# First batch of a fused attention and two-expert-layer kernel: transposes first, the second weight matrix converted between the last pieces of the first, loads put behind the first product

## The chip, the cores and the metric

The kernel runs on 1 core of one Trainium2 chip. The metric is the device time of a run in microseconds; lower is better. The engines are written as the profile writes them: PE (TensorE), DVE (VectorE), ACT (ScalarE), POOL (GpSimd), SP (SyncE, which here only issues DMAs). Each engine works through its own list of instructions in order.

## The reference

Eight batches of 576 tokens go through a Nystrom attention (8 heads of 64, 32 landmarks), then through a dense layer with squared ReLU, then through a layer of 8 experts of which each token takes one:

```
q_lm, k_lm = means of q and k over 18 rows each          # 32 landmarks
A, Bm, C = softmax(q k_lm'), softmax(q_lm k_lm'), softmax(q_lm k')
Z = iterated inverse of Bm (6 rounds)
x = A @ Z @ C @ v                                         # 4608 x 512
h = relu(x @ w_in); x = (h * h) @ w_out                   # w_in 512 x 2048, w_out 2048 x 512
e = argmax(x @ w_gate)
out = softmax gate * sigmoid(x @ w_output_gate)[e] * (relu(x @ w1[e]) @ w2[e])
```

The inputs w_in, w_out, w1 and w2 arrive as 64-bit floats in DRAM.

## The kernel before

All large products are made with three matmuls of 32-bit operands: a high part times a high part, and two cross terms. A value is split into a high part (ACT copies it into the rounded type `F32R`) and a low part (DVE or POOL subtracts).

For each batch b the attention leaves a matrix A (`made`, split into `ab`) and a weight `wt` made from Z, C and v. `chunk` multiplies `wt` into w_in, a quarter of its columns at a time; the four products of a batch are called G (`gt`, tiles `gb`). `gemm(b)` then runs over two halves c of the batch's tokens (288 columns each) and over 16 slices f of the hidden width: six matmuls give `hp`, ACT makes `r = relu(hp)`, `gh` and `g` (both the square of r, one rounded, one not), DVE makes `gl = g - gh`, and `second` multiplies w_out's slice f (`wo`) with gh and gl: twelve matmuls into `acc`. `second` runs two slices behind `hp`.

Everything for batch 0 has to happen before that. `prologue` loads q and k (tiles `t`), makes their landmark sums (`sums`: on DVE, for the last tile on POOL, tile `st`), transposes q and k on PE (`transposed`, ACT copies the result to `x`), and runs the steps of `unit` for batch 0: landmarks (`lm`), scores, softmaxes (`ec`, `aa`), values, the powers of the inverse (`ee`, `ef`), the last values (`wz`) and `wt`. `first_g` then makes the first two G.

Between these steps `convert` turns w_in and w_out from 64 to 32 bits, in 16 pieces of 128 x 512 for each: a DMA fetches `raw` (four buffers), a cast makes the top half word `m` (on ACT or on POOL), ACT makes `r` from the low words, POOL adds the two in two halves into `wf` (w_in) or `w` (w_out). A piece of w_in is written back to DRAM (`win`) for the later batches. A piece of w_out is split as soon as it is converted: ACT copies, DVE subtracts, into `wo[f]`.

The steps of the next batch's attention run beside `gemm` as side work, `rate` steps for each of the four points of a slice; a scheduler at build time decides the order on each engine. It takes hints: `high_priority`, and `follow(a, b)`, which puts a behind b in the order without making it wait on the chip. The DMAs of loads and write-backs are issued by SP in order.

## Time and profile before

| | |
|---|---|
| time, median of 3 runs | 1259.56 us (1258.18 to 1260.97) |
| the profiled execution's own time | 1259.2 us |
| its span | 1257.5 us |
| PE busy | 1206.7 us, 96% of the span |
| DVE, ACT, POOL busy | 591.3, 615.2, 421.3 us |
| mean granted clock of PE | 0.978 of full speed |

The span is the time from the first to the last instruction; 1.7 us of the profiled execution lie around it. "Busy" is the time in which an engine had an instruction in work; waiting on another engine is not busy.

### The profile page before, as it was taken

How to read it: one execution, taken by the hardware profiler on the slowest of the kernel's cores; microseconds unless marked ns; L12 is line 12 of the kernel's file. 1: busy time of each engine (PE TensorE's matmuls, PEld its weight loads, DVE VectorE, ACT ScalarE, POOL GpSimd, SP SyncE). 2: the span in 40 equal slices, each digit the busy share in tenths (PEclk: the TensorE clock that was granted, in tenths of full speed). 3: DMA queues.
4: the chain of work that ended last, by engine and by line, in shares of the span. 5: the costliest groups of instructions: out<-in, count | busy, mean ns of one | idle time of the engine just before them, and what ended most of it. 6: DMA issues, size and time to landing. Idle time of an engine off the chain costs nothing.

```text
span 1257.5 us, 25149 instructions
## 1 busy us (share of the span) xinstructions
PE 1206.7 (96%) x9834; PEld 1078.6 (86%) x9834; DVE 591.3 (47%) x1498; ACT 615.2 (49%) x1433; POOL 421.3 (34%) x568
## 2 busy tenths in 40 slices
PE   4598999999999999999999999999999999999996
PEld 3377888989989989989989999998888888888885
DVE  5586466567547557556556332233333323323231
ACT  5586364564564564564564454553343433424331
POOL 5787514332233233232112000163342423424220
PEclk7699999999999999999999999999999999999998
DMA  9944333252152142141133210152534435343231
GB/s 339 336 164 135 124 122 109 91 168 61 59 171 64 53 158 77 53 158 58 54 120 108 69 37 2 39 151 84 143 105 139 129 115 159 108 125 110 90 96 40
DMA packets 88408, 142.24 MB, mean 113 GB/s; under 512 B 6430, under 2 KB 61758, under 8 KB 84702
## 3 DMA queue, kind: packets, MB, share of 16 engines
q1 hardware_dynamic: 87854, 139.97, 34.4%
q8 instruction: 79, 1.29, 0.4%
q0 software_dynamic: 288, 0.43, 0.1%
q14 instruction: 43, 0.35, 0.1%
q10 hardware_dynamic: 144, 0.20, 0.0%
HBM read 117.47 MB, written 23.11 MB: 112 GB/s over the span
## 4 chain that ended last, share of the span: by engine, by line
PE 90%; DVE 3%; DMA 3%; ACT 2%; POOL 1%; issue 1%; SPq 0%; POOLq 0%; ACTq 0%; DVEq 0%
PE acc L402 32%; PE hp L402 32%; PE y L402 17%; PE two L398 4%; PE bank L398 2%; PE bank L410 1%; DMA raw<-in_moe_w_in_dram 1%; PE pl L398 1%; DMA v<-in_v_dram 1%; PE pt L1168 1%; DVE x L488 1%; DMA t<-in_q_dram 1%; DVE gl L1079 1%; ACT r L185 0%; DVE ma L559 0%
## 5 line engine op out<-in xcount | busy, mean ns | idle before, releaser
L402 PE MATMUL acc<-gh,wo 128*128 128x288 f32 x2048 | 453.5, 299 | 7.7 <-ACT wo L218 5.0
L402 PEld LDWEIGHTS acc<-gh,wo 128*128 128x128 f32 x2048 | 341.1, 189 | 30.0 <-ACT gh L1077 8.4
L402 PE MATMUL acc<-gl,wo 128*128 128x288 f32 x1024 | 288.9, 298 | 1.1 <-DVE gl L1079 1.1
L402 PE MATMUL hp<-ab,gb 128*128 128x288 f32 x1536 | 255.7, 301 | 1.6 <-ACT r L1076 1.5
L402 PEld LDWEIGHTS hp<-ab,gb 128*128 128x128 f32 x1536 | 216.0, 189 | 21.3 <-issue 11.8
L1076 ACT ACTIVATE r<-hp 128x288 f32<-128x288 f32 x256 | 105.4, 412 | 256.0 <-PE hp L402 254.4
L1079 DVE TENSOR_TENSOR gl<-g,gh 128x288 fp32r<-128x288 f32 x256 | 131.4, 514 | 198.8 <-ACT g L1078 192.6
L402 PE MATMUL y<-s,h 128*128 128x512 f32 (+1 forms) x896 | 223.0, 396 | 0.8 <-ACT h L1311 0.5
L402 PEld LDWEIGHTS hp<-xs,s 128*128 128x128 f32 x1536 | 212.2, 188 | 7.5 <-DVE ls L1522 0.3
L402 PE MATMUL hp<-xs,s 128*128 128x288 f32 x1536 | 217.1, 295 | 0.2 <-DVE ls L1522 0.2
L402 PEld LDWEIGHTS acc<-gl,wo 128*128 128x128 f32 x1024 | 193.4, 189 | 4.0 <-DVE gl L1079 3.0
L402 PEld LDWEIGHTS y<-s,h 128*128 128x128 f32 (+1 forms) x896 | 160.6, 184 | 37.7 <-ACT h L1311 0.7
L230 POOL TENSOR_TENSOR s<-r,s 128x256 fp32r<-128x256 f32 x128 | 102.0, 819 | 234.8 <-ACT s L218 234.8
L1311 ACT ACTIVATE h<-hp 128x288 fp32r<-128x288 f32 x128 | 52.6, 412 | 186.8 <-PE hp L402 172.6
L1314 DVE SCALAR_TENSOR_TENSOR h<-hp,h 128x64 fp32r<-128x64 f32 (+2 forms) x192 | 62.6, 354 | 166.3 <-ACT h L1311 165.9
L1077 ACT ACTIVATE gh<-r 128x288 fp32r<-128x288 f32 x256 | 114.2, 446 | 12.5 <-PE acc L402 5.8
L1078 ACT ACTIVATE g<-r 128x288 f32<-128x288 f32 x256 | 110.6, 432 | 5.3 <-DVE gl L1079 5.0
L218 ACT CAST s<-r 128x512 fp32r<-128x512 f32 x128 | 77.6, 617 | 71.4 <-PE y L402 56.1
L499 POOL COPY x<-x 32x576 f32<-32x576 f32 x48 | 33.9, 706 | 195.7 <-DVE x L488 102.7
L224 DVE TENSOR_TENSOR s<-r,s 128x512 fp32r<-128x512 f32 x64 | 50.9, 795 | 103.3 <-ACT s L218 103.3
L230 POOL TENSOR_TENSOR xs<-xr,xs 128x576 fp32r<-128x576 f32 x32 | 45.9, 1459 | 64.0 <-ACT xs L218 48.0
L444 POOL TENSOR_TENSOR st<-t 128x288 f32<-128x288 f32 x50 | 40.7, 835 | 75.1 <-DMA t<-in_q_dram 73.1
(198 smaller groups left out, 1097.7 us busy)
## 6 DMA issues: line engine op xcount, KB each, us to landing
r<-in_moe_w_dram SPq DMA_DIRECT2D x128, 256.0 KB
wi<-win SPq DMA_DIRECT2D x28, 1024.0 KB
t<-in_k_dram SPq DMA_DIRECT2D x16, 576.0 KB
t<-in_q_dram SPq DMA_DIRECT2D x16, 576.0 KB
v<-in_v_dram SPq DMA_DIRECT2D x32, 288.0 KB
x_d<-x SPq DMA_DIRECT2D x16, 576.0 KB
xr<-x_d SPq DMA_DIRECT2D x16, 576.0 KB
raw<-in_moe_w_in_dram SPq DMA_DIRECT2D x16, 511.8 KB
```

What stands on the lines that cost most here:

```text
L218: hi = self.nc.scalar.copy(out=t[:, 0], in_=raw)
L224: lo_eng.tensor_tensor(out=t[:, 1], in0=raw, in1=t[:, 0].bitcast(F32), op=ALU.subtract)
L230: self.nc.gpsimd.tensor_tensor(out=out[:, p], in0=in0[:, p], in1=in1[:, p], op=op)
L398: self.in_run(lambda: self.nc.tensor.matmul(out, **kw))
L402: mm = self.nc.tensor.matmul(out, **kw)
L444: add = lambda out, in0, in1: self.nc.gpsimd.tensor_tensor(out=out, in0=in0, in1=in1, op=ALU.add)
L1076: nc.scalar.activation(out=r, in_=hp[:, 0:HC], func=ACTF.Relu)
L1077: nc.scalar.activation(out=gh, in_=r, func=ACTF.Square)
L1078: nc.scalar.activation(out=g2, in_=r, func=ACTF.Square)
L1079: nc.vector.tensor_tensor(out=gl, in0=g2, in1=gh.bitcast(F32), op=ALU.subtract)
L1311: nc.scalar.activation(out=h[:, t0:t1], in_=hp[:, 0:HC], func=ACTF.Relu)
L1314: nc.vector.scalar_tensor_tensor(out=h[:, to + a:to + z], in0=hp[:, a - t0:z - t0], scalar=0.0, in1=h[:, a:z].bitcast(F32), op0=ALU.max, o ...
```

## The change

- The steps of batch 0: all landmark sums come first (k, k, q, q, the last on POOL ahead of q's first), then all twelve transposes, six groups for k and six for q. Before, q's transposes ran beside the inverse. ACT instead of POOL doubles the sums in this batch, and makes two of the four `wz` copies instead of DVE.
- The order of conversion: eight pieces of w_in, two of w_out, then one of w_in and one of w_out by turns, then the rest of w_out. All pieces of w_in that stand at an even place have their cast on ACT (12 in place of 8).
- Where it is converted to: w_out's piece f gets a slot of its own (`wb`), kept whole until `split_out` splits it at the slice that uses it. The high part goes into the slot of w_in's piece f (`wa`), the low part into the slot of the piece before. So the high part of f waits until w_in's piece f has been read by G and written back to DRAM.
- Behind the first G in the order (`paced`): the write-backs of w_in, the loads of the next batch's q, k and v. v of batch 0 is loaded after the sixth step.
- In the first half of batch 0, DVE makes the unrounded square (`r * r`) instead of ACT; the third and fourth G come at f = 4 and 8 in place of 2 and 4; side work runs at 0.2 and 0.9 steps a point in the two halves in place of 0.3 and 0.8.
- Three buffers in place of two for `m` and `r`; 13 pieces of w_in instead of 14 at most before the first G.

```
-CONV_BUFS = 2
+CONV_BUFS = 3
-CONV_EARLY = 14
+CONV_EARLY = 13
-RATES = {(0, 0): 0.3, (0, 1): 0.8}
+RATES = {(0, 0): 0.2, (0, 1): 0.9}
...
-            if i < 4 * KD and i % 2 == 0:
-                nc.scalar.activation(out=top, in_=high, func=ACTF.Copy)
+            ops = []
+            if jobs[i][3] and i % 2 == 0:
+                ops.append(nc.scalar.activation(out=top, in_=high, func=ACTF.Copy))
...
-                lambda w: self.hold(lambda: self.nc.sync.dma_start(out=self.win_d[n][:, kp], in_=w)),
+                lambda w: self.hold(lambda: self.paced(self.nc.sync.dma_start(out=self.win_d[n][:, kp], in_=w))),
...
-                self.wo[f] = self.wop.tile([128, 2, DM], F32R, tag=f"wo{f}", name="wo")
-                self.split(self.wo[f], w, self.nc.vector)
...
+    def weights_order(self):
+
+        i, o = self.convert_in(), self.convert_out()
+        first, rest = i[:G_FIRST * KD], i[G_FIRST * KD:]
+        jobs = first + o[:2]
+        for k, w in enumerate(rest):
+            jobs += [w, o[2 + k]]
+        return jobs + o[2 + len(rest):]
+
+    def split_out(self, last):
+
+        while len(self.wo) <= min(last, NFC - 1):
+            f = len(self.wo)
+            while f not in self.whole:
+                next(self.conv)
+            while self.g_done <= f // KD:
+                self.first_g_of(self.g_done)
+            w = self.whole[f]
+            hi = self.wop.tile([128, 512], F32R, tag=f"wa{f}", name="hi")
+            lo = self.wop.tile([128, 512], F32R, tag=f"wb{f}", name="lo")
+            self.nc.scalar.copy(out=hi, in_=w)
+            self.nc.vector.tensor_tensor(out=lo, in0=w, in1=hi.bitcast(F32), op=ALU.subtract)
+            self.wo[f] = hi, lo
...
+    def paced(self, op):
+
+        if self.last_h is not None or self.last_gb is not None:
+            self.follow(op, self.last_h or self.last_gb)
...
-        if u["pe"]:
+        if u["early"]:
+            for nm, hg in (("k", 0), ("k", 1), ("q", 1), ("q", 0)):
+                self.sums(u, nm, hg)
+            for nm in "kq":
+                for hg, i in both:
+                    self.transposed(u, nm, hg, i)
+                    yield STEP
...
-            yield from weave(self.sooner(weave(cv_alone(), self.powers(u))), itertools.chain(tq(), a()))
+            yield from weave(self.sooner(weave(cv_alone(), self.powers(u))), a())
...
-                if (b, c) == (0, 0) and f > 0 and f % 2 == 0 and self.g_done < min(4, f // 2 + G_FIRST):
+                if (b, c) == (0, 0) and f % 4 == 0 and self.g_done < min(4, f // 4 + G_FIRST):
                     self.first_g_of(self.g_done)
+                if (b, c) == (0, 0):
+                    self.split_out(f)
...
-                    nc.scalar.activation(out=g2, in_=r, func=ACTF.Square)
+                    if (b, c) == (0, 0):
+                        nc.vector.tensor_tensor(out=g2, in0=r, in1=r, op=ALU.mult)
+                    else:
+                        nc.scalar.activation(out=g2, in_=r, func=ACTF.Square)
```

What the change does to the order on SP, from the loads of v for batch 0 (`v`) on. Before, write-backs (`win`) and the next batch's loads (`t`) stand between the fetches of w_in:

```order
L434 DMA v<-in_v_dram 96x2x384 x4
L170 DMA raw<-in_moe_w_in_dram 128x2047
L425 DMA t<-in_k_dram 128x1152 x2
L170 DMA raw<-in_moe_w_in_dram 128x2047
L244 DMA win_112<-wf 128x512
L170 DMA raw<-in_moe_w_in_dram 128x2047 x2
L244 DMA win_112<-wf 128x512 x2
L170 DMA raw<-in_moe_w_in_dram 128x2047
```

Now no write-back stands there; they come later, from these rows on, with w_out's fetches and the next batch's loads between them:

```order
L171 DMA raw<-in_moe_w_in_dram 128x2047
L446 DMA t<-in_k_dram 128x1152
L246 DMA win_112<-wf 128x512 x2
L446 DMA t<-in_k_dram 128x1152
L246 DMA win_112<-wf 128x512
L171 DMA raw<-in_moe_w_out_dram 128x2047
L246 DMA win_112<-wf 128x512
L446 DMA t<-in_q_dram 128x1152
L246 DMA win_113<-wf 128x512
```

Ahead of these rows there are now only batch 0's own loads and 21 fetches, 14 of w_in and 7 of w_out; no write-back and no load of the next batch.

POOL, from the sums of the last q tile (`st`, `sums`) to the second half of the softmax (`aa`), which A and then `wt` stand behind. Before, the stretch begins as follows, and goes on in this pattern:

```order
L444 TENSOR_TENSOR sums<-st 128x128
L230 TENSOR_TENSOR wf<-m,r 128x256 x4
L184 CAST m<-raw 128x512
L230 TENSOR_TENSOR wf<-m,r 128x256 x4
L184 CAST m<-raw 128x512
```

Now the whole stretch:

```order
L470 TENSOR_TENSOR sums<-st 128x128
L232 TENSOR_TENSOR wf<-m,r 128x256 x2
L186 CAST m<-raw 128x512
L232 TENSOR_TENSOR wf<-m,r 128x256 x4
L186 CAST m<-raw 128x512 x2
L232 TENSOR_TENSOR wf<-m,r 128x256 x6
L186 CAST m<-raw 128x512 x2
L232 TENSOR_TENSOR wf<-m,r 128x256 x2
L232 TENSOR_TENSOR aa<-aa,ma 128x288 x2
L232 TENSOR_TENSOR w<-m,r 128x256 x4
L232 TENSOR_TENSOR aa<-aa,ma 128x288 x2
```

Before, 25 adds of conversion and 6 casts stood between `sums` and the last `aa`; now 18 and 5 do. Ahead of `sums` stand four adds instead of two, and one cast as before.

ACT, from the first `r` of a slice on. Before:

```order
L1076 ACTIVATE r<-hp 128x288
L1077 ACTIVATE gh<-r 128x288
L1078 ACTIVATE g_806<-r 128x288
L473 COPY x<-bank 128x3x4x32
L1019 CAST gb<-two 128x512
L1076 ACTIVATE r<-hp 128x288
```

Now:

```order
L1114 ACTIVATE r<-hp 128x288
L1115 ACTIVATE gh<-r 128x288
L284 CAST hi<-w 128x512
L187 ACTIVATE r<-raw 128x512
L1055 CAST gb<-two 128x512
L284 CAST hi<-w 128x512
L1114 ACTIVATE r<-hp 128x288
```

The split of w_out's slice 0 (`hi`) now stands behind the first slice's `r` and `gh`, and the second slice's `r` behind the splits of slices 0 and 1; the unrounded square is gone from this list.

## Rows read from the trace of the kernel before

**Rows 1.** Windows: stretch, its length, busy time (instructions) by engine, clock, DMA share, GB/s.

```profile
10.00:50.00 40.00, 20.81 (x420) 13.08 (x420) 17.73 (x60) 23.28 (x48) 28.58 (x42) 0.60 1.04 359
...
70.00:110.00 40.00, 36.79 (x389) 31.84 (x387) 23.96 (x49) 34.33 (x83) 30.38 (x39) 1.00 0.53 178
110.00:130.00 20.00, 14.17 (x110) 12.20 (x106) 19.45 (x35) 10.30 (x23) 18.11 (x25) 1.00 0.22 68
130.00:140.00 10.00, 9.90 (x65) 8.94 (x65) 4.33 (x11) 3.65 (x10) 9.22 (x15) 0.83 0.83 316
140.00:1257.50 1117.50, 1105.32 (x8726) 999.29 (x8724) 502.54 (x1299) 526.09 (x1237) 314.75 (x413) 1.00 0.31 96
```

The engines in these rows are PE, PE's weight loads, DVE, ACT and POOL, in that order.

**Rows 2.** Groups of ACT, 9 to 50.5 us: busy us, mean ns, idle before and releasers.

```profile
L185 ACT ACTIVATE r<-raw 128x512 int32<-128x512 uint32 x15 | 9.8, 658 | 6.3 <-DMA raw<-in_moe_w_in_dram 6.3
L182 ACT ACTIVATE m<-raw 128x512 f16<-128x512 bf16 x8 | 6.3, 786 | 8.1 <-DMA raw<-in_moe_w_in_dram 5.1 <-POOL wf L230 2.7 <-POOL m L184 0.3
```

**Rows 3.** Timeline up to the first G: start, duration, instruction, idle before and its releaser.

```profile
16.41 0.46 POOL L444 TENSOR_TENSOR sums<-st 128x128 f32<-128x128 f32 x1
...
46.03 0.68 ACT L565 ACTIVATE aa<-aa 128x576 f32<-128x576 f32 x1
...
46.74 0.75 DVE L567 TENSOR_REDUCE ma<-aa 128x18 f32<-128x576 f32 x1 [2.35 <-ACT aa L565]
...
50.71 3.67 PE L398 MATMUL bank<-wf,wt 64*32 64x512 f32 x32 [0.89 <-ACT wt L816]
```

**Rows 4.** Timeline: the first `acc`, and the first `r` of three halves.

```profile
61.43 0.42 ACT L1076 ACTIVATE r<-hp 128x288 f32<-128x288 f32 x1
...
63.51 1.16 PE L402 MATMUL acc<-gh,wo 128*128 128x288 f32 x4
...
113.34 0.41 ACT L1076 ACTIVATE r<-hp 128x288 f32<-128x288 f32 x1
...
173.69 0.41 ACT L1076 ACTIVATE r<-hp 128x288 f32<-128x288 f32 x1 [0.37 <-PE hp L402]
```

**Rows 5.** PE's waits from 55 to 140 us: total us, times, longest us.

```profile
PE acc L402 <- ACT wo L218: 5.0, 6, 1.9
...
PE acc L402 <- DVE wo L224: 2.6, 2, 1.7
```

**Rows 6.** Groups of POOL from 9 to 50 us.

```profile
L230 POOL TENSOR_TENSOR wf<-m,r 128x256 int32<-128x256 int32 x26 | 18.2, 725 | 7.7 <-ACT r L185 7.3
L184 POOL CAST m<-raw 128x512 f16<-128x512 bf16 x7 | 5.8, 826 | 2.1 <-DMA raw<-in_moe_w_in_dram 2.0
...
L230 POOL TENSOR_TENSOR aa<-aa,ma 128x288 f32<-128x288 f32 x2 | 1.3, 670 | 0.0
```

**Rows 7.** DMA issues up to 60 us, by line: count and size of one.

```profile
raw<-in_moe_w_in_dram SPq DMA_DIRECT2D x16, 511.8 KB
win<-wf SPq DMA_DIRECT2D x15, 256.0 KB
...
t<-in_k_dram SPq DMA_DIRECT2D x4, 576.0 KB
```

**Rows 8.** Groups of DVE from 61 to 113 us.

```profile
L224 DVE TENSOR_TENSOR wo<-w,wo 128x512 fp32r<-128x512 f32 x13 | 11.3, 866 | 9.0 <-ACT wo L218 9.0
L1079 DVE TENSOR_TENSOR gl<-g,gh 128x288 fp32r<-128x288 f32 x14 | 8.4, 602 | 5.3 <-ACT gh L1077 3.6 <-ACT g L1078 1.6
L455 DVE TENSOR_REDUCE sums<-t 128x32 f32<-128x576 f32 x5 | 5.6, 1173 | 0.1
L1020 DVE TENSOR_TENSOR gb<-two,gb 128x512 fp32r<-128x512 f32 x4 | 2.7, 682 | 0.1
...
L685 DVE TENSOR_SCALAR bc<-bank,mc 128x64 f32<-128x64 f32 x2 | 0.6, 278 | 1.0 <-PE bank L398 1.0
```

**Rows 9.** The large matmuls of PE (L402) alone, 150 to 160 us.

```profile
150.00:160.00 10.00, 9.60 (x69) 9.11 (x69) 1.00 0.01 2
```

**Rows 10.** The subtraction `gl` after 140 us: least, median and greatest duration in ns.

```profile
L1079 DVE TENSOR_TENSOR gl<-g,gh x235: 393/459/1079, 140.4 to 829.9; 128x288 fp32r<-128x288 f32 x118
```

More of the change, by code (lines that the diff above doesn't have):

```diff
@@ L40 @@
 CONV_AHEAD = 4
-CONV_BUFS = 2
-CONV_EARLY = 14
+CONV_BUFS = 3
+CONV_EARLY = 13
 CONV = 0.45
 CONV_SOON = 0.8
+V_LATE = 6
 CONV_FIRST = 2
@@ L101, in __init__ @@
         self.gt, self.at, self.made, self.g_done, self.last_gb, self.last_lo = {}, {}, {}, 0, None, None
-        self.held = []
+        self.held, self.whole = [], {}
         self.wf, self.wo, self.qk, self.vt, self.wts, self.wis = {}, {}, {}, {}, {}, {}
@@ L180, in scale @@
             high = raw.bitcast(BF16).rearrange("p (n t) -> p n t", t=4)[:, :, 2]
-            if i < 4 * KD and i % 2 == 0:
-                nc.scalar.activation(out=top, in_=high, func=ACTF.Copy)
+            ops = []
+            if jobs[i][3] and i % 2 == 0:
+                ops.append(nc.scalar.activation(out=top, in_=high, func=ACTF.Copy))
             else:
                 nc.gpsimd.tensor_copy(out=top, in_=high)
-            first = nc.scalar.activation(
+            ops.append(nc.scalar.activation(
                 out=r, in_=raw.rearrange("p (n t) -> p n t", t=2)[:, :, 0].bitcast(U32), func=ACTF.Copy,
                 scale=2.0 ** -13,
-            )
+            ))
             if self.last_gb is not None:
-                self.follow(first, self.last_gb)
+                self.follow(ops[0], self.last_gb)
             st[i] = m, r
@@ L237, in place @@
             def place():
[L238 removed]
+                self.wf[i] = self.wop.tile([128, 512], F32, tag=f"wa{i}", name="wf")
                 return self.wf[i]
@@ L251, in job @@
         def job(f):
-            def parts(w):
-                while self.g_done <= f // KD:
-                    self.first_g_of(self.g_done)
-                self.wo[f] = self.wop.tile([128, 2, DM], F32R, tag=f"wo{f}", name="wo")
-                self.split(self.wo[f], w, self.nc.vector)
             return (
                 self.w_out[f * 128:(f + 1) * 128, :],
-                lambda: self.cv.tile([128, 512], F32, tag="cw", name="w", bufs=CONV_BUFS),
-                parts,
+                lambda: self.wop.tile([128, 512], F32, tag=f"wb{f + 1}", name="w"),
+                lambda w: self.whole.update({f: w}),
+                False,
             )
         return [job(f) for f in range(NFC)]
+    def weights_order(self):
[18 more added lines that the diff above has]
+            self.wo[f] = hi, lo
     def run(self):
@@ L433, in load_v @@
             for a in range(2):
-                self.nc.sync.dma_start(out=t[:, 2 * a:2 * a + 2], in_=src[a, g])
+                self.paced(self.nc.sync.dma_start(out=t[:, 2 * a:2 * a + 2], in_=src[a, g]))
     def sums(self, u, nm, hg):
-        if hg == 0:
+        if nm + "s" not in u:
             u[nm + "s"] = self.sm.tile([128, 2, 2, D], F32, tag=f"{nm}s", name="sums", bufs=1)
@@ L446, in sums @@
             for c in range(0, 2 * n, n):
-                add(x[:, c:c + n], t[:, c:c + n], t[:, 2 * n + c:3 * n + c])
+                self.paced(add(x[:, c:c + n], t[:, c:c + n], t[:, 2 * n + c:3 * n + c]))
             for w in (256, 128, 64):
@@ L459, in sums @@
                 self.follow(total, self.last_lo)
-        self.nc.gpsimd.tensor_copy(out=s[:, 1], in_=s[:, 0])
+        (self.nc.scalar.copy if u["early"] else self.nc.gpsimd.tensor_copy)(out=s[:, 1], in_=s[:, 0])
     def transposed(self, u, nm, hg, i):
         if i == 0:
-            u[nm, hg] = self.tp.tile([128, 4, 9, LM], F32, tag="xT", name="x", bufs=2)
+            pool = u["early"] if u["early"] and nm == "q" else self.tp
+            u[nm, hg] = pool.tile([128, 4, 9, LM], F32, tag="xT", name="x", bufs=2)
         t = self.qk[nm, u["b"], hg]
@@ L799, in last_values @@
         for j in range(4):
-            self.nc.vector.tensor_copy(out=self.crossed(wz, j), in_=w[32 * j:32 * j + 32])
+            copy = self.nc.scalar.copy if j % 2 else self.nc.vector.tensor_copy
+            copy(out=self.crossed(wz, j), in_=w[32 * j:32 * j + 32])
     def diagonal(self, u, x):
@@ L936, in prologue @@
         self.constants()
-        conv = self.conv = self.convert(self.convert_in() + self.convert_out())
+        conv = self.conv = self.convert(self.weights_order())
         next(conv)
-        self.load_v(0, 0)
-        self.load_v(0, 1, early)
         due = 0.0
@@ L943, in prologue @@
         work = self.unit(u)
-        while True:
+        for i in itertools.count():
             with self.tc.high_priority(URGENT):
@@ L949, in prologue @@
             self.tick(False)
+            if i == V_LATE:
+                self.load_v(0, 0)
+                self.load_v(0, 1, early)
             due += CONV if len(self.wf) >= G_FIRST * KD else CONV_SOON
@@ L1086, in gemm @@
                         pass
+                    self.split_out(NFC - 1)
                     self.conv = None
@@ L1099, in second @@
         nc = self.nc
-        while f not in self.wo:
-            next(self.conv)
+        self.split_out(f)
         if f == 0:
@@ L1109, in second @@
                 self.big(
-                    acc[m][:, 0:HC], lhsT=self.wo[f][:, l, ms], rhs=r,
+                    acc[m][:, 0:HC], lhsT=self.wo[f][l][:, ms], rhs=r,
                     start=(f == 0 and i == 0), stop=(f == NFC - 1 and i == 2),
```

7 lines of the change are left out of this document (4 added, 3 removed).

## Prediction

> **What bounds the kernel now.** I read the windows first. After 140 us PE is busy for 1105.32 of 1117.5 us [rows 1]: it works through its list and waits for almost nothing, so whatever the change gains or loses before that point stays to the end, and nothing behind it can give it back. What can be won lies ahead of it. From 10 to 50 us PE is busy 20.81 of 40 us at a granted clock of 0.60 [rows 1], on the small matmuls of batch 0's attention; from 110 to 130 us it is idle 20 - 14.17 = 5.8 us, and the clock of the ten microseconds behind that is 0.83.
>
> Next, why the first stretch is slow. The 16 DMA engines are taken for all of it (share 1.04, 359 GB/s [rows 1]), and ACT, whose conversion steps stand in one queue with the attention's, waits 6.3 and 5.1 us for fetched pieces [rows 2]. The timeline shows what hangs on that: the second exponential of the softmax starts only at 46.03, DVE has waited 2.35 us for it, and the first G starts at 50.71 [rows 3]. The first `acc` follows at 63.51; the first half of batch 0 lasts from 61.43 to 113.34, 51.9 us, and the second from there to 173.69, 60.35 us [rows 4]. In that time PE waits eight times, 7.6 us in all, for the split of a piece of w_out [rows 5].
>
> **The change, term by term.**
>
> *1, the first G.* The queue to count is POOL's, since the second half of the softmax product (`aa`) stands on it and A and `wt` stand behind that. Before, the last sums ended at 16.41 + 0.46 = 16.9 [rows 3]. Now two more adds stand ahead of them, 2 x 0.725 [rows 6]: 18.3. From there to the end of `aa` there are 18 adds, 5 casts and 4 halves of `aa`: 18 x 0.725 + 5 x 0.826 + 4 x 0.670 = 19.9 [rows 6], so 38.2 if POOL never waits. Before it waited 7.3 us in this stretch for ACT's `r` [rows 6], which waited for fetches [rows 2]. Of the transfers of the first 60 us, 15 write-backs of 256 KB and two of the four loads of k [rows 7] are now behind the first G: 15 x 0.262 + 2 x 0.590 = 5.1 MB, at 359 GB/s 14 us of the engines' time. What is left of the wait lies between nothing and 7.3; I take a third, 2.4, because the fetches still go through four buffers that ACT empties in its own order: 40.6. The last leg, from the second exponential to G, took 50.71 - 46.03 = 4.7 [rows 3]; now it holds the transposes of `aa`, the last two rounds of the powers, `wz` and `wt`, and I leave it at 4.7. First G at 45.3, **-5.4 us**; the bounds are 42.9 (-7.8) and 50.2 (-0.5). That all sums and transposes come first costs nothing by itself: ACT's copies end before the last sums do, and the transposes that stood between the powers are gone from there.
>
> *2, the first half of batch 0.* DVE gets sixteen squares and loses none of its work. Its list from the first `r` to the last holds 16 squares and 16 `gl`, 13 splits, 4 `gb`, 8 reductions for the next batch, some 14 small instructions. The square is not in the trace of before; I price it as `gl`, which has the same shape and two inputs from SBUF: 602 ns [rows 8]. 32 x 0.602 + 13 x 0.866 + 4 x 0.682 + 8 x 1.173 + 14 x 0.278 = 46.5 us [rows 8]. ACT loses 16 squares and its conversions go on at the same count, so DVE is the longest list. PE's own floor: 288 large matmuls at 9.60 / 69 = 0.139 [rows 9] are 40.1, with the side work some 43. So the half takes 46.5 in place of 51.9, **-5.4**; the floor would be -8.9.
>
> The `gl` of this stage is slow for a reason: after 140 us the median is 459 ns, with single ones up to 1079 [rows 10], against a mean of 602 here, where POOL is busy three quarters of the time (30.38 of 40 [rows 1]). The Trainium skill, SBUF — State Buffer, section "SBUF: two separate sides", says that DVE and POOL share a pair of ports, and that a DVE instruction with two SBUF inputs and a POOL instruction that reads SBUF lock each other out for a whole instruction. The spread in the rows agrees. It speaks against moving the squares: by it each of them can stand behind a POOL add, or hold one up; if all did, the first rival below would be the forecast.
>
> *3, the side work moved.* 64 points times 0.1 are 6.4 steps out of the first half, where they save nothing while DVE is the limit, into the second. The second half now: 60.35 less 288 x 0.139, less 5.8 idle and 1.7 lost to the clock (0.17 x 10 [rows 1]), leaves 12.7 for 0.8 x 64 = 51 steps, 0.25 each. **+1.6**; at least nothing.
>
> *4, the second half.* Its 5.8 idle and 1.7 of slow clock [rows 1] come while the last pieces of w_out are converted and split and the next batch's softmax shares DVE (19.45 of 20 busy) and POOL (18.11). Now POOL's last conversion add stands ahead of that softmax's products, so the waits on w_out go [rows 5]; but the DVE work of the softmax stays, and the inverse's rounds stand two to a slice instead of one. I take half, **-3.75**; bounds 0 and -7.5.
>
> *5, the first splits.* The high part of slice 0 waits until w_in's first piece is written back. Ahead of this write SP has two fetches (2 x 0.524 MB), a load of k (0.590) and the write itself (0.262): 1.9 MB, 5.3 us at 359 GB/s, from an issue that comes after the first two `gb`, some 4 us behind G. So slice 0 can be split about 10 us behind G. The first `acc` came 63.51 - 50.71 = 12.8 behind it, so `acc` need not be later; but ACT is in order, and while it stands at this split, the second slice's `r`, two `gb` and three conversions stand behind it. The first `r` comes some 3 us earlier relative to G than before (no late `gb` ahead of it), ACT and DVE then stand some 4, and a DVE list of 46 us is not run without waits: 2 more. **+3**, bounds -3 and +6.
> By the Trainium skill, DMA: Bandwidth & Descriptors, section "Anatomy of one DMA — SWDGE (gpsimd) path", the receipt of a write to HBM takes most of about 2 us; no row here shows a wait for a write-back, and with it the sum would be 2 us later.
>
> Sum: -5.4 - 5.4 + 1.6 - 3.75 + 3 = -9.95 on the profiled execution's 1259.2, so 1249.25; the median lies 0.36 above that execution: **1249.6**.
>
> **The rivals.**
>
> *DVE against POOL (slower).* Only the first half changes sign. Without term 2 the sum is -4.55. With x for the mean of `gl` and square, and splits in proportion (0.866 / 0.602 = 1.44), DVE's list is 50.7 x + 16.0. It decides at x = 0.86, where the half takes 59.6 and the whole comes 0.25% late; the greatest single one is 1.079. At x = 1.0 the half takes 66.7: 14.8 - 4.55 = +10, 1270. For it: the locks of the rows, and three POOL steps to a slice. Against: the mean of 602 was measured beside the same POOL work. Chance 0.08.
>
> *No earlier G.* ACT and POOL still convert 15 pieces ahead of `wt`, as before, and this, not the DMA engines, set the time: G at 50.2. Then -0.5 in place of -5.4: 1254.5. For it: POOL is busy 28.58 of 40 us. Against: ACT's 11.4 us of waiting on fetches. Chance 0.2.
>
> *All waits go.* PE's floor in the first half and the whole of term 4: -5.4 - 8.9 + 1.6 - 7.5 + 3 = -17.2, 1242.4. For it: the conversions are one to three slices ahead. Against: DVE. Chance 0.15.
>
> *A wash.* The early start is eaten by the first splits (term 5 at +6) and the second half's waits stay: -5.4 - 5.4 + 1.6 + 6 = -3.2, or less where term 1 falls short too: 1256.4 to 1260. Chance 0.12.
>
> **How the numbers follow.** The forecast holds 0.45. Less than 0.2% (2.5 us) cannot be told from no change here. Faster by more: the forecast, all waits gone, no earlier G nearly whole, and some of the wash: 0.82. Same: 0.09, from the wash. Slower: 0.09, the DVE rival and its edge. The range leaves out half of "all waits go" below and the DVE rival with the end of the wash above: 1243 to 1258.
>
> **What would show it.** Right: the first G near 45 us, SP's write-backs behind it, ACT no longer waiting for fetches ahead of it; the first half near 46 us with DVE nearly full; no wait of `acc` on w_out after the first slices. Wrong: `hi` waiting for DMAs through several slices with PE behind it; squares and `gl` near 0.9 us; the idle of PE between 110 and 130 still there, a few microseconds earlier; or a first G at 50.

## Result, and the profile after

The changed kernel takes **1269.15 us** (median of 6 runs, 1266.7 to 1273.75), the kernel before 1259.84 (6 runs beside it): ratio 1.0077, 95% interval 1.0056 to 1.0098, so 0.8% slower, where 1249.6 was forecast. Its profiled execution is the slowest of its runs: 1273.75 us, span 1272.0; so 4.6 us of what the profile below shows are not in the median.

Windows of the changed kernel, cut at the first `r` of each stage (first five slices of batch 0, the other eleven, nine slices of the second half, the last seven, and ten microseconds in batch 2); the columns are those of [rows 1]:

```profile
57.57:80.58 23.01, 17.97 (x104) 14.43 (x105) 20.57 (x26) 13.71 (x31) 13.27 (x16) 0.85 1.03 382
80.58:114.78 34.20, 30.43 (x250) 26.64 (x248) 29.38 (x50) 23.78 (x56) 27.39 (x34) 1.00 0.38 128
114.78:146.70 31.92, 30.17 (x276) 27.75 (x277) 9.25 (x23) 16.94 (x42) 1.85 (x3) 1.00 0.39 141
146.70:181.03 34.33, 30.45 (x261) 26.40 (x260) 25.69 (x57) 12.83 (x32) 19.00 (x30) 0.85 0.30 95
290.00:300.00 10.00, 5.52 (x80) 4.05 (x78) 1.42 (x3) 2.23 (x6) 0.00 (x0) 0.69 0.75 194
```

The kernel before, cut in the same way (five slices, eleven; then five and eleven of the second half):

```profile
61.43:76.32 14.89, 14.31 (x98) 12.11 (x96) 11.92 (x16) 11.80 (x31) 10.45 (x15) 0.85 0.66 239
76.32:113.34 37.02, 34.23 (x370) 29.70 (x371) 23.03 (x49) 30.70 (x74) 29.24 (x37) 1.00 0.51 165
113.34:139.13 25.79, 20.02 (x141) 17.12 (x140) 20.16 (x37) 10.81 (x25) 23.19 (x35) 0.93 0.41 152
139.13:173.69 34.56, 34.56 (x304) 31.73 (x304) 15.67 (x48) 17.70 (x46) 5.57 (x9) 1.00 0.17 62
```

The start is won: the first `r` stands at 57.57 in place of 61.43. Then it is lost in three places. The first five slices take 23.0 us instead of 14.9, with DVE busy 20.57 of them. In the second half DVE (9.25 of 31.9) and POOL (1.85) have little to do for nine slices; then seven slices take 34.3 us, in which PE waits 3.9 us and works at a clock of 0.85. And PE, which in the kernel before had no wait for a DMA after 140 us, is idle 4.5 us in batch 2, at 0.69 of its clock in these ten microseconds.

The timeline of the changed kernel at the three places that answer to [rows 3, 4] (first G, first `r`, first split, second `r`):

```profile
47.16 3.67 PE L419 MATMUL bank<-wf,wt 64*32 64x512 f32 x32 [0.35 <-ACT wt L844]
...
57.57 0.40 ACT L1114 ACTIVATE r<-hp 128x288 f32<-128x288 f32 x1
...
61.02 0.62 ACT L284 CAST hi<-w 128x512 fp32r<-128x512 f32 x1 [2.59 <-DMA win<-wf]
...
63.10 0.41 ACT L1114 ACTIVATE r<-hp 128x288 f32<-128x288 f32 x1
```

DVE's groups in the first half (57 to 115 us), which answer to [rows 8]:

```profile
L285 DVE TENSOR_TENSOR lo<-w,hi 128x512 fp32r<-128x512 f32 x14 | 13.3, 948 | 0.1
L1117 DVE TENSOR_TENSOR g<-r 128x288 f32<-128x288 f32 x16 | 12.0, 750 | 5.8 <-ACT r L1114 5.7
L1120 DVE TENSOR_TENSOR gl<-g,gh 128x288 fp32r<-128x288 f32 x15 | 11.7, 783 | 1.6 <-ACT gh L1115 0.8
L481 DVE TENSOR_REDUCE sums<-t 128x32 f32<-128x576 f32 x8 | 9.2, 1186 | 1.6 <-DMA t<-in_k_dram 1.6
```

The square takes 750 ns, not 602; `gl` went from 602 to 783, the split from 866 to 948. Of the eight sums six now lie in the first five slices (four before). In the kernel before the first six stood in one block, most of it ahead of the first `r`:

```profile
57.01 6.50 DVE L455 TENSOR_REDUCE sums<-t 128x32 f32<-128x576 f32 x6
```

The rounds of batch 1's inverse, by their first instruction on DVE:

```profile
157.22 0.38 DVE L834 TENSOR_TENSOR dg<-bank,h 128x256 f32<-128x256 f32 x1
...
168.54 0.42 DVE L834 TENSOR_TENSOR dg<-bank,h 128x256 f32<-128x256 f32 x1 [0.55 <-PE bank L419]
```

These are the first and the last of five; in the kernel before they stand at:

```profile
139.49 0.43 DVE L806 TENSOR_TENSOR dg<-bank,h 128x256 f32<-128x256 f32 x1 [1.33 <-PE bank L398]
...
152.90 0.42 DVE L806 TENSOR_TENSOR dg<-bank,h 128x256 f32<-128x256 f32 x1 [1.71 <-PE bank L398]
```

Behind the rounds comes batch 1's first G, and behind that the half ends. In the changed kernel batch 1's first `r` (181.03) follows this G by 8.1 us, in the kernel before (173.69) by 13.2:

```profile
172.96 1.09 PE L419 MATMUL two<-wi,wt 64*32 64x512 f32 x16 [0.36 <-ACT wt L844]
```

```profile
160.50 1.09 PE L398 MATMUL two<-wi,wt 64*32 64x512 f32 x16
```

And the wait in batch 2 (SP's issues and the two steps that read v):

```profile
280.63 0.55 SPq L1174 DMA_DIRECT2D x_d<-x  x1
281.98 0.33 SPq L1041 DMA_DIRECT2D wi<-win  x1
282.40 1.52 SPq L446 DMA_DIRECT2D t<-in_q_dram  x1
...
283.07 0.88 PE L419 MATMUL bank<-v,et 96*32 96x64 f32 x48
284.02 1.08 SPq L460 DMA_DIRECT2D v<-in_v_dram  x2
...
288.20 0.34 SPq L1041 DMA_DIRECT2D wi<-win  x1
...
295.53 1.51 PE L419 MATMUL bank<-v,et 96*32 96x64 f32 x48 [4.48 <-DMA v<-in_v_dram]
```

There is one buffer for both halves of v: the second is loaded only when the first half's step has been done, and is needed by the next such step. Here 11.5 us passed between its issue and its use. Two loads of 1 and 0.59 MB and a write of 0.59 MB had been issued ahead of it, another load of 1 MB followed at 288.20, and the DMA engines were busy for nearly all of that time (share 0.97, 274 GB/s):

```profile
284.02:295.53 11.51, 7.03 (x60) 5.83 (x61) 3.12 (x6) 3.84 (x9) 0.00 (x0) 0.93 0.97 274
```

### The profile page after: what moved, and what is told of

It reads as the page before. It is cut to its first block, busy times and chain, and to the rows that moved or that the text cites. A ratio compares the mean times of both kernels' runs of the same rounds, so it can differ in the third digit from the quotient of the medians.

```text
span 1272.0 us, 25140 instructions
## 1 busy us (share of the span) xinstructions
PE 1217.9 (96%) x9834; PEld 1085.6 (85%) x9834; DVE 604.4 (48%) x1512; ACT 613.0 (48%) x1426; POOL 419.2 (33%) x562
## 4 chain that ended last, share of the span: by engine, by line
PE 89%; DVE 6%; DMA 2%; ACT 1%; issue 1%; POOL 0%; SPq 0%; POOLq 0%; DVEq 0%; ACTq 0%
PE hp L423 31%; PE acc L423 30%; PE y L423 16%; PE two L419 4%; PE bank L419 3%; PE bank L431 1%; DVE sums L481 1%; DMA v<-in_v_dram 1%; PE pl L419 1%; DVE gl L1120 1%; DVE x L515 1%; DMA t<-in_k_dram 1%; PE pt L1209 1%; DMA raw<-in_moe_w_in_dram 1%; DVE g L1117 1%
## 5 line engine op out<-in xcount | busy, mean ns | idle before, releaser
L423 PE MATMUL acc<-gl,hi 128*128 128x288 f32 x1024 | 290.1, 301 | 4.2 <-DVE gl L1120 4.1
L423 PE MATMUL acc<-gh,lo 128*128 128x288 f32 x1024 | 283.3, 297 | 2.6 <-DVE lo L285 2.6
L1120 DVE TENSOR_TENSOR gl<-g,gh 128x288 fp32r<-128x288 f32 x256 | 134.1, 524 | 222.6 <-ACT g L1119 214.0
L423 PE MATMUL acc<-gh,hi 128*128 128x288 f32 x1024 | 210.4, 299 | 2.0 <-ACT hi L284 2.0
L423 PEld LDWEIGHTS acc<-gl,hi 128*128 128x128 f32 x1024 | 193.6, 189 | 13.6 <-DVE gl L1120 6.1
L423 PEld LDWEIGHTS acc<-gh,lo 128*128 128x128 f32 x1024 | 192.3, 189 | 4.3 <-DVE lo L285 3.3
L423 PEld LDWEIGHTS acc<-gh,hi 128*128 128x128 f32 x1024 | 160.4, 189 | 11.1 <-ACT gh L1115 3.8
L1119 ACT ACTIVATE g<-r 128x288 f32<-128x288 f32 x240 | 103.3, 430 | 0.9 <-DVE gl L1120 0.9
L226 DVE TENSOR_TENSOR s<-r,s 128x512 fp32r<-128x512 f32 x64 | 50.7, 792 | 102.1 <-ACT s L220 102.1
```

What stands on the lines that cost most here:

```text
L226: lo_eng.tensor_tensor(out=t[:, 1], in0=raw, in1=t[:, 0].bitcast(F32), op=ALU.subtract)
L423: mm = self.nc.tensor.matmul(out, **kw)
L1119: nc.scalar.activation(out=g2, in_=r, func=ACTF.Square)
L1120: nc.vector.tensor_tensor(out=gl, in0=g2, in1=gh.bitcast(F32), op=ALU.subtract)
```

## The experiments

All numbers in one table: median of the runs, and from the profiled execution the first G, the first `r`, the two halves of batch 0 (first `r` to first `r`), and what follows to the end of the span. The last five columns are of one execution each. Up to the first G the order on every engine is the same in changed, e1, e3, e4, e5, e11 and e12, and yet it stands between 46.7 and 48.7 in them; so up to 2 us in that column is scatter.

| kernel | median us (runs) | first G | first r | half 1 | half 2 | rest |
|---|---|---|---|---|---|---|
| before | 1259.84 (6) | 50.7 | 61.4 | 51.9 | 60.3 | 1083.8 |
| changed | 1269.15 (6) | 47.2 | 57.6 | 57.2 | 66.2 | 1091.0 |
| e1 square on ACT | 1267.10 (5) | 47.4 | 56.8 | 52.9 | 64.6 | 1087.6 |
| e2 before, square on DVE | 1263.22 (7) | 50.2 | 60.9 | 54.1 | 60.9 | 1084.3 |
| e3 old rates | 1262.71 (11) | 47.3 | 56.4 | 52.9 | 63.7 | 1087.4 |
| e4 later loads unpaced | 1270.60 (6) | 47.0 | 56.2 | 56.7 | 62.9 | 1090.7 |
| e5 = e1 + e3 | 1258.08 (11) | 47.4 | 56.6 | 53.0 | 60.2 | 1086.4 |
| e6 e3 + own slot | 1262.81 (11) | 49.1 | 57.2 | 53.4 | 62.6 | 1086.7 |
| e7 before, new rates | 1260.51 (12) | 51.2 | 62.0 | 52.1 | 53.8 | 1095.6 |
| e8 e5 + own slot | 1258.55 (11) | 48.4 | 56.3 | 53.6 | 59.5 | 1086.7 |
| e9 e7 + second v buffer | **1252.05** (5) | 51.3 | 62.1 | 52.2 | 54.9 | 1083.2 |
| e10 before + second v buffer | 1256.11 (5) | 51.2 | 62.0 | 52.3 | 55.6 | 1084.7 |
| e11 changed + second v buffer | 1264.68 (6) | 46.7 | 56.0 | 57.6 | 65.2 | 1085.0 |
| e12 e1 + second v buffer | 1263.11 (8) | 48.7 | 57.7 | 52.4 | 64.7 | 1086.5 |
| e13 loads unpaced | 1261.88 (12) | 48.2 | 58.7 | 58.5 | 52.1 | 1088.0 |
| e14 e5 + loads unpaced | 1257.49 (11) | 47.5 | 58.6 | 58.8 | 51.3 | 1086.2 |
| e15 e12 + loads unpaced | 1258.05 (11) | 47.3 | 58.2 | 58.8 | 52.1 | 1087.1 |
| e16 e15, old rates | 1257.68 (11) | 47.9 | 59.1 | 58.4 | 51.3 | 1086.8 |
| e17 e16, sums behind gl | 1256.20 (6) | 48.1 | 59.6 | 54.2 | 55.1 | 1085.9 |
| e18 e9, write-backs paced | 1258.99 (12) | 52.4 | 63.6 | 53.4 | 57.0 | 1083.3 |

### The square (e1, e2)

e1, in the changed kernel (e2 makes the opposite edit in the kernel before):

```
-                    if (b, c) == (0, 0):
-                        nc.vector.tensor_tensor(out=g2, in0=r, in1=r, op=ALU.mult)
-                    else:
-                        nc.scalar.activation(out=g2, in_=r, func=ACTF.Square)
+                    nc.scalar.activation(out=g2, in_=r, func=ACTF.Square)
```

> The changed kernel with the unrounded square of batch 0's first half back on ACT; nothing else is edited. Theory 'DVE too long': the first half (57.2 us, from the first r to the first r of the second half) is set by DVE, whose instructions there take 0.75 us (square), 0.78 (gl) and 0.95 (split) in place of the 0.60 and 0.87 of the forecast, 49.9 us busy of 57.2. Without 16 squares of 0.75 DVE is busy some 38 us, ACT some 44.5, and the half falls to 51 to 53: 4 to 6 us faster than the changed kernel, 1263 to 1265. Rival 'late splits': the half is set by the splits of w_out, which wait on ACT for write-backs at its start, and by ACT's order; ACT then has 7 us more and the half stays at 56 to 59: 1268 to 1271.

> The kernel before with the one edit that DVE makes the unrounded square in batch 0's first half. Theory 'DVE too long': DVE goes from 35 us busy to 48 to 50 of a half that lasted 51.9, ACT from 42.5 to 35.5; DVE becomes the longest list, with POOL's conversions beside it: the half gets 1 to 4 us longer, 1261 to 1264. Rival 'late splits' (DVE's work costs nothing as long as the list is shorter than the half): the half stays or gets shorter because ACT is freed: 1257 to 1260.

The first half did in both runs what "DVE too long" says: 57.2 to 52.9 in e1, 51.9 to 54.1 in e2, where the time followed (1263.22; ratio 1.0031, 1.002 to 1.0042). In e1 the time didn't: 1267.10 lies between the two ranges. DVE's rows of e2's first half:

```profile
L224 DVE TENSOR_TENSOR wo<-w,wo 128x512 fp32r<-128x512 f32 x13 | 12.2, 936 | 3.7 <-issue 1.6 <-ACT wo L218 1.5 <-DMA t<-in_q_dram 0.7
L1079 DVE TENSOR_TENSOR g<-r 128x288 f32<-128x288 f32 x16 | 11.8, 739 | 0.8 <-ACT r L1076 0.6
L1082 DVE TENSOR_TENSOR gl<-g,gh 128x288 fp32r<-128x288 f32 x14 | 9.3, 664 | 3.2 <-ACT gh L1077 2.6
```

So the square costs 739 ns, and `gl` and the split get longer with it (602 to 664, 866 to 936). The median of e1 fell by 2 us only. Its profile, the fastest of its runs, doesn't say why; it has 1.4 us of waiting for v, and its first half is no shorter than 53, although DVE's busy time went from 50 to 36. The later runs bound what the square does. With the old rates the first half is the same with and without it (52.9 in e3, 53.0 in e5), and so it is with the loads back (58.5 in e13, 58.8 in e14 and e15). In the median it costs 1.6 us (e11 to e12) to 4.6 (e3 to e5).

### The rates (e3, e5, e7)

```
-RATES = {(0, 0): 0.2, (0, 1): 0.9}
+RATES = {(0, 0): 0.3, (0, 1): 0.8}
```

> The changed kernel with the old rates of side work, 0.3 and 0.8 steps a point in batch 0's two halves. The second half lasts 66.3 us in the changed kernel against 60.4 before. Theory 'the steps moved are what the second half gained': 6.4 steps come back into the first half, the rounds of the inverse no longer wait in sequence late in the second half with PE at the low clock behind them (granted clock 0.62 from 160 to 170 us): second half 61 to 63, the first half 1 to 2 us longer because DVE is full there: 1265 to 1268. Rival 'the steps cost the same in either half': 1268 to 1271.

> The changed kernel with both edits taken back: the square of the first half on ACT, and side work at 0.3 and 0.8 steps a point. Taken back alone they gave 1267.1 (2.05 us less than the changed kernel's 1269.15) and 1262.7 (6.4 less). Theory 'two causes, which add': 1260 to 1261.5. Rival 'both relieve the same first half' (it fell from 57.2 to 52.9 us with either edit, to 52.89 with the one and 52.92 with the other, and PE's own matmuls and ACT's list of 41 to 45 us leave little below that): the second edit gives 1.5 us at most over the old rates alone, 1261.5 to 1263.

> The kernel before with the new rates alone, 0.2 and 0.9 steps a point. Theory 'the moved steps cost by themselves': the rounds of the inverse come late in the second half, where each waits for DVE between two of PE's groups; 3 to 6 us slower than before, 1263 to 1266. Rival 'they cost only because DVE is full in the changed kernel's first half and the steps were late already': 0 to 2 us slower, 1260 to 1262, which is the 1.6 us of the forecast's third term.

e3 gained 6.4 us, more than either theory gave, and in places that neither named: the first half lost 4.3 us although it got more side work, and no wait for v is left. e5 gained more than the sum of e1 and e3 (11.1 against 8.5 us), so both its theories missed, and it ends below the kernel before (ratio 0.9987, 0.9979 to 0.9996). In e7 the median agrees with the rival and its reason doesn't: the second half is 6.5 us *shorter*, and the rest 11.8 longer. The runs go from 1256.54 to 1265.28, and the profiled one is the slowest, so the median has less of that. The waits of PE behind batch 0 in e7:

```profile
PE bank L398 <- DMA v<-in_v_dram: 8.4, 4, 3.8
```

and two neighbouring steps that read v, 11.65 us apart where the kernel before has 18.4 (274.49 to 292.85):

```profile
272.60 0.88 PE L398 MATMUL bank<-v,et 96*32 96x64 f32 x48
...
273.54 0.94 SPq L434 DMA_DIRECT2D v<-in_v_dram  x2
...
284.25 0.88 PE L398 MATMUL bank<-v,et 96*32 96x64 f32 x48 [3.78 <-DMA v<-in_v_dram]
```

### v in two buffers (e9 to e12), and later loads without pacing (e4)

e4 took the pacing of q, k and v away once w_out is converted:

> The changed kernel, but loads of q, k and v are put behind the last hp only as long as w_out is being converted; from batch 1's second half on they stand where they stood before. In the profiled execution of the changed kernel PE waits 4.48 us at 291 us for a load of v that was issued at 284.02, right behind a load of q at 282.40 and one of w_in's product at 281.98, and its clock falls to 0.69 behind it. Theory 'paced loads bunch up': the loads of q come earlier, v does not queue behind them, this wait and the clock go: 3 to 6 us faster than the profiled execution, 2 to 5 in the median, 1264 to 1267. Rival 'the wait is a matter of when the steps fall, not of the pacing': another load of v is as late, 1268 to 1271.

The rival held: PE waits 5.8 us for v, in four places, so the pacing isn't what makes these waits. Behind batch 0 all waits for v stand between steps 7 to 13 us apart, and at 14.8 us or more there is none. But a short distance alone doesn't make one: in every other batch of the changed kernel the two steps are 8 us apart, and PE doesn't wait:

```profile
380.70 0.88 PE L419 MATMUL bank<-v,et 96*32 96x64 f32 x48
...
388.66 0.88 PE L419 MATMUL bank<-v,et 96*32 96x64 f32 x48
```

e9 to e12 give the second half of v a buffer of its own:

```
             def swap():
                 tmp.close()
                 self.wi = T("wi", 2)
+                self.v1 = T("v1")
...
         if (b, 1) not in self.vt:
-            self.load_v(b, 1)
+            self.load_v(b, 1, self.v1)
         elif hg == 1:
             self.hold(lambda: self.load_v(b + 1, 0))
+            if b > 0:
+                self.load_v(b + 1, 1, self.v1)
```

> The kernel before with the new rates, and with a buffer of its own for the second half of v of each later batch (opened when the conversion's buffers are closed), loaded as soon as the batch ahead has used it, instead of one buffer for both halves. With the new rates alone, batch 1 began at 167.90 us against 173.69 in the kernel before, and yet the median was 1260.5 with a spread from 1256.5 to 1265.3; the two steps that use v stood 7 to 11 us apart in place of 17 to 23, and PE waited four times, 8.4 us, for the second half of v, which can be loaded only once the first half's step is done. Theory 'the moved steps put v's second load on the path': without it the 5.8 us of the first batch stay: 1252 to 1256, spread under 4. Rival 'later batches pay for the other order anyway': 1258 to 1262.

> The kernel before with only the second buffer of v. PE waits for no load of v there. Theory 'v on the path only with the new rates': no change, 1258.5 to 1260.5. Rival 'another buffer helps the loads behind it too, whatever the rates': 1254 to 1257.

> The changed kernel with the second buffer of v. In its profiled execution PE waits 4.48 us for v at 291 us and then works at a clock of 0.69; its runs spread from 1266.7 to 1273.75. Theory 'v on the path': the half of batch 2 goes from 57.8 to 51 or 52 us in the profile; in the median 3 to 5 us less, 1264 to 1266, spread under 4. Rival 'the order of the side steps costs it': 1267.5 to 1270.

> The changed kernel (new rates) with the square back on ACT and the second buffer of v. The square alone gave 1267.1; of its runs the profiled one, 1263.63, had 1.4 us of waiting for v, the others lie at 1266.9 to 1268.0. Theory 'v on the path': 1261 to 1263.5, all runs near the fastest of the square alone. Rival: 1265.5 to 1268.

"v on the path" held in e9, e11 and e12: no wait for v is left, the spread of e9 is 1251.61 to 1254.1. (That of e11 is 5.4 us, where under 4 was expected.) e9 is the fastest kernel of this study, 1252.05 (ratio to before 0.9939, 0.9926 to 0.9952). For the changed kernel the waits were worth 4.5 us of the median (1269.15 to 1264.68), and 6.0 of the profiled execution's rest. In e10 the theory missed, and the rival had the time and not the reason: it gained 3.7 us with no wait to take away. Its second half fell from 60.3 to 55.6: batch 1's second v, now in memory that conversion uses first, is loaded at 122.4 in place of 110.1, and the softmax products of batch 1 begin on POOL at 136.0 in place of 113.8. In the kernel before they and the inverse stood among the last splits (PE idle 5.8 us there [rows 1]). In e7 the new rates do the same (134.5).

### The loads of the next batch (e13 to e17)

e13, in the changed kernel (the same for v):

```
-        self.paced(self.nc.sync.dma_start(
+        self.nc.sync.dma_start(
             out=t.rearrange("p s d -> p (s d)"), in_=src.rearrange("h (l s) d -> (h l) (s d)", s=SEG)
-        ))
+        )
```

> The changed kernel, but all loads of q, k and v stand where they stood before (only w_in's write-backs stay behind the first G). Theory 'late loads push batch 1 back': its sums (at 60, 65, 72 and 92 us in the changed kernel, 57 and 66 before) come 10 to 25 us earlier, with them the rounds of its inverse, which in the changed kernel run one after another at 157 to 169 us, shortly before batch 1's G needs them; the second half goes from 66.3 to 58 to 61 us and the first loses 1 to 2: 1260 to 1264. Rival 'the new rates and DVE set it': the second half stays at 64 to 66, 1266 to 1270.

> The changed kernel with the square on ACT, the old rates and the loads unpaced. Without the last edit: 1258.1, first G 47.4, halves 53.0 and 60.2. Theory 'late loads push batch 1 back': second half 56 to 58, 1254 to 1256.5. Rival 'the loads cost the first G what they give behind it' (three loads of 0.59 MB before it are 5 us at 359 GB/s): first G 2 to 3 us later, 1258 to 1261.

> The changed kernel (new rates) with the square on ACT, the loads unpaced and the second buffer of v. Without the unpaced loads: 1263.1, halves 52.4 and 64.7. Theory 'late loads': second half 55 to 58 as in the kernel before with these rates (53.8 and 54.9), 1253 to 1256. Rival: second half above 62, 1261 to 1264.

> The same with the old rates: square on ACT, loads unpaced, second buffer of v. Every cause found is taken back, and what is left of the change is its order of the prologue, of the conversion and of the write-backs. Theory: the 4 to 5 us by which batch 0's first r comes earlier stay, and the second half is 55 to 57: 1250 to 1254, level with or below the 1252.05 of the kernel before with new rates and second buffer. Rival 'the changed conversion costs a few us of the halves by itself': 1255 to 1259.

The time of e13 lies in its theory's range, its halves don't. The second fell by 14.2 us, and in e13 to e16 it is 51 or 52: the late loads held batch 1 back, by more than the theory gave. The rounds of its inverse now begin at 144.55 in place of 157.22:

```profile
144.55 0.41 DVE L834 TENSOR_TENSOR dg<-bank,h 128x256 f32<-128x256 f32 x1
```

The median gains less, and the less the more of the other edits are taken back already: 7.3 us alone, 5.1 on top of e12 (e15), 0.6 on top of e5 (e14). Windows of e13, the two halves:

```profile
58.67:117.14 58.47, 52.59 (x391) 43.10 (x384) 48.64 (x83) 41.80 (x94) 42.33 (x48) 0.97 0.69 236
117.14:169.20 52.06, 50.62 (x496) 45.42 (x495) 29.69 (x68) 24.79 (x60) 23.66 (x36) 1.00 0.27 88
```

But the first half did not shrink, it grew, to 58.4 or more with the square on either engine, and so e14 and e15 missed both of their figures and e16 came out with the rival. DVE's timeline in e13 shows a reason: all six sums ahead of the first split, and ahead of the first slice's square, whose `r` ended at 59.1:

```profile
55.83 6.54 DVE L481 TENSOR_REDUCE sums<-t 128x32 f32<-128x576 f32 x6
62.29 0.69 DVE L285 TENSOR_TENSOR lo<-w,hi 128x512 fp32r<-128x512 f32 x1
```

e17 puts the sums behind the newest gl:

```
-                    nc.vector.tensor_tensor(out=gl, in0=g2, in1=gh.bitcast(F32), op=ALU.subtract)
+                    low = nc.vector.tensor_tensor(out=gl, in0=g2, in1=gh.bitcast(F32), op=ALU.subtract)
+                self.last_lo = low
```

> As e16 (square on ACT, old rates, loads unpaced, second buffer of v), and the next batch's sums in this stage are put behind the gl of the slice that is current, not only behind the low part of G. Theory 'the six sums ahead of the first gl hold the first half up': they take 7 us at 55.9 there, PE waits 4 us for gl; without it the first half goes from 58.4 to 52 to 54 and the second stays at 51 to 54: 1251.5 to 1255. Rival 'the splits and conversions fill the half anyway': first half 56 to 58, 1256 to 1258.5.

The first half fell from 58.4 to 54.2, the upper end of that theory; the second gave most of it back (51.3 to 55.1), and the time, 1256.20, is the rival's, 1.5 us below e16. Together the halves take 109.3 against 112.3 before. So the place of the six sums is worth 4.2 us of the first half; it isn't the whole cause, since the kernel before has the same block at 57.01 and a first half of 51.9.

### The first splits and the write-backs (e6, e8, e18)

e6 and e8:

```
-            hi = self.wop.tile([128, 512], F32R, tag=f"wa{f}", name="hi")
+            hi = self.wop.tile([128, 512], F32R, tag=f"wa{f - 1}" if f else "wh", name="hi")
```

> The changed kernel with the old rates, and with a slot of its own for the high part of w_out's slice 0, so that slice f's high part goes into the slot of w_in's piece f - 1: slice 0 waits for no write-back, the others for one piece earlier. With the old rates alone ACT waits 3.20 us at the first split for the write-back, from 57.25 to 60.45, and the second r, queued behind it, starts 6.16 us after the first. Theory 'the first splits hold ACT up': the second r comes 3 us sooner, and what PE then does earlier stays: 1259.5 to 1260.7. Rival 'it only moves the wait' (the two write-backs are issued together, so slice 1 waits in slice 0's place, and DVE, busy 46.2 of 52.9 us, is the longer list anyway): 1262 to 1263.5.

> The changed kernel with all three: square on ACT, old rates, and the slot of its own for slice 0's high part. Theory 'three causes, which add': 1257 to 1259.5, not slower than the kernel before. Rival 'what the earlier start gave is used up behind it anyway' (with the old rates batch 1 began at 173.0 against 173.7 before, and yet the end came 2.9 us later): 1260 to 1263.

No gain over e3 and e5: the wait moves to slice 1, as e6's rival had it. (The time of e8 lies in its theory's range, but so does e5's without the slot.) In e8 the wait is 3.69 us, and the second `r` comes 7.0 us after the first:

```profile
61.19 0.62 ACT L284 CAST hi<-w 128x512 fp32r<-128x512 f32 x1 [3.69 <-DMA win<-wf]
```

e18 paces only the write-backs, in e9:

```
-                lambda w: self.hold(lambda: self.nc.sync.dma_start(out=self.win_d[n][:, kp], in_=w)),
+                lambda w: self.hold(lambda: self.paced(self.nc.sync.dma_start(out=self.win_d[n][:, kp], in_=w))),
```

> The kernel before with the new rates and the second buffer of v (1252.05), and w_in's write-backs put behind the first G. First G at 51.33 without them. Theory 'the write-backs held the first G up' (13 of them, 3.4 MB, 9.5 us of the DMA engines at 359 GB/s): G at 47 to 49, the halves unchanged but for the first splits, which share their slots with w_in's pieces: 1248.5 to 1251. Rival 'the fetches go at ACT's pace anyway, and the first splits wait for the late write-backs': G at 50 to 51, first half 1 to 3 us longer, 1252 to 1255.

It went past the rival: first G at 52.38, no earlier, both halves longer, 7 us slower than e9. Its first five slices take 18.5 us where those of e9 take 15.3, with DVE busy 12.1 of them.

## Why the prediction was wrong, step by step

In the profiled executions the change costs 14.5 us: -3.9 to the first `r`, +5.3 in the first half, +5.9 in the second, +7.2 behind it (1091.0 less 1083.8). In the medians it costs 9.3.

**The step that failed most** is the second half: terms 3 and 4 sum to -2.15 there, and it got 5.9 longer. They price the next batch's work as time on an engine and ask nowhere when it is due, and term 1 counts the late loads only as room on the DMA engines. The sums, scores and softmax of batch 1 hang on these loads, and the inverse behind them is a chain of rounds between PE and DVE. It started 18 us later and ran into the G that needs it, with little left beside it. The idle time of PE that term 4 wanted to halve only moved: 1.8 and 3.9 us in the two parts of the half, where 5.8 stood. The low clock grew: 0.15 of 34.3 us, by estimate 5 us, where it was 0.07 of 25.8, by estimate 2.

e13 shows it: with the loads back, and nothing else, the rounds begin 12.7 us sooner, the second half is 14.2 us shorter, and the median falls by 7.3. But the loads are not the only cause. With the loads still late, the square on ACT and the old rates (e5) give a second half of 60.2, as before, and a median of 1258.08. The first `r` of batch 1, at 181.0 in the changed kernel, comes 11.8 us sooner in e13, 11.2 in e5, and 12.4 with both (e14). So three edits delay the same chain, and what they cost overlaps: taken back alone they give 2.1 (square), 6.4 (rates) and 7.3 us (loads) of the median. Which of the three weighs most is not settled.

Nor is later always worse. The softmax products of batch 1 begin on POOL at 113.8 in the kernel before, among the last splits, and the second half takes 60.3. At 134 to 137 (e7, e9, e10, e13 to e17) it takes 51 to 56, from 139 on (e5, e3, e1) 60 to 65, and at 151.1, in the changed kernel, 66.2.

**Term 1** had the sign and less of the size: G at 47.16, not 45.3. But POOL's list, from which it was added up, is not what G waited for, and `wt` doesn't need `aa`. In the kernel before, the copy of `wt` stood on ACT right behind two steps of conversion, which waited for a fetch:

```profile
49.23 0.78 ACT L182 ACTIVATE m<-raw 128x512 f16<-128x512 bf16 x1 [0.62 <-DMA raw<-in_moe_w_in_dram]
49.87 0.63 ACT L185 ACTIVATE r<-raw 128x512 int32<-128x512 uint32 x1
50.41 0.25 ACT L816 COPY wt<-bank 128x128 f32<-128x128 f32 x1
```

In the changed kernel the last fetch in the chain that ends in G landed at 21.4, and no work of POOL stands behind it. From 24 us on the chain runs through the softmax on DVE and ACT, then through the powers on PE and DVE (pieces of it: start, length, what):

```profile
14.86 6.54 DMA raw<-in_moe_w_in_dram
...
38.92 2.59 PE bank L419 x88
...
44.11 0.23 DVE ef L808
...
46.85 0.27 ACT wt L844
```

POOL waited 5.2 us for ACT and fetches between its sums and the end of `aa`, where I took 2.4. That the last leg came out at 4.7, as taken, is luck, since it starts at `aa`. In e11, whose order up to G is the same, the chain goes through fetches, ACT and single adds of POOL up to 44 us, and G stands at 46.70; so two paths are nearly level, and `aa` is on neither. What brought G forward was not separated: write-backs behind G alone (e18) bring it no forward, and with the next batch's loads back (e13) it stands at 48.19, within the scatter. What is left is the order on the engines, sums and transposes first, alone or together with these transfers; that wasn't tried.

**Term 2** (-5.4) took the half to be as long as DVE's list. The list was mis-sized: the square and `gl` have a mean of 0.77 us, not 0.602, the split 0.948, not 0.866. In the rival's formula that is 50.7 x 0.77 + 16.0 = 55 us, so more than the 51.9 it had to beat. The half was longer than the list as well: DVE was busy 49.95 us of 57.2 (20.57 and 29.38), and idle the rest. The rival's deciding point, 0.86, was not reached, since it was set by a sum whose other terms were wrong too. POOL's additions grew as well (822 to 913 ns between the same stages). The Trainium skill, SBUF — State Buffer, section "SBUF: two separate sides", has DVE's two-input instructions and POOL's that read SBUF lock each other out; lengthening on both engines agrees, and it spoke against the square rightly. e1 and e2 show that the square makes the first half 2 to 4 us longer in these two kernels. With the old rates or with the loads back it doesn't; yet from e3 to e5 the median falls by 4.6 us without it, so there its price lies behind the first half.

**Term 5** (+3, bounds to +6) was too small. The waits are of the kind described (2.6 us for the write-back in the first five slices, and PE 0.9 for a late load of k), but these slices lost 8.1 us. e6 and e8 moved the write-back's wait and did not remove it, so they don't tell what it costs. A full DVE isn't the cause alone either: in e1 these slices still take 22.1 us, and DVE is busy 17.5 of them. In e17, without both waits and with the sums put behind `gl`, they take 19.2, where 14.9 stood. The other 4.3 us stay open; e18, where only the write-backs came late, lost 3.2 there.

**Term 3** (+1.6) had the wrong sign for the kernel before (e7: second half 6.5 us shorter), since side work that is kept out of the end of the conversion lets PE's waits there go (PE idle 5.8 us from 110 to 130 in the kernel before, 2.2 in e7). In the changed kernel, where batch 1 is late already, it cost 2.5 (e3) to 4.4 us (e1 to e5) of the second half, and with the loads back less than one (e15 to e16).

**"Nothing behind it can give it back"** was read from PE's busy share after 140 us, and is wrong: another rate in batch 0 shifts the side work of all later batches against their G, and in batch 2 the two steps that use v came so close that the second load no longer fits between them. With the second buffer of v the rest is 1085.0 in the changed kernel.

**Open:** with all waits for v gone, every kernel built on the changed one still has 1.2 to 3.6 us more behind batch 0 than the kernel before, with PE nearly always busy. These are single executions, and no run separates a cause.

## What to carry to other kernels

Before a load is moved back to make room, follow what hangs on it to its next deadline: here the deadline was a serial chain a whole stage later. When several edits delay the same chain, taking back one alone doesn't tell its share. An instruction that goes to another engine is not to be priced at the mean that its neighbours had without it, since it also slows these. And a buffer that is refilled between two uses can turn into a wait when an edit elsewhere brings the uses closer; here a second buffer took that wait away in each of the three kernels that had it and were given one.

## What the runs showed of the hardware

A load of v (590 KB) took 11.5 us from issue to use behind 1 and 0.59 MB that had been issued 2.0 and 1.6 us ahead, where all three are 6 us at the 359 GB/s of [rows 1]. The difference is not idle time: the DMA engines were at a share of 0.97, moved 274 GB/s, and had a write ahead of the three and another load behind them in hand. That the later load held the earlier one up is likely and not shown.

Waits at such an edge differ from place to place in one execution (3.78, 0.73, 3.47 and 0.41 us in e7), and e7's runs spread over 8.7 us, e9's, with the wait taken away, over 2.5. That the wait makes the spread is not shown: e11 has none, and spreads over 5.4.

And 4.5 us without work cost PE more than that: its granted clock was 0.50 (1.2 GHz) from 294 to 300 us, and 0.69 in the ten microseconds around the wait.
